# Turning rows by transfers through DRAM and VectorE's 32x32 transposition instead of by TensorE, in a fused attention, MLP and mixture-of-experts kernel

## The chip, the cores and the metric

The kernel runs on one core of a Trainium2 chip. The metric is the device time of one execution in microseconds (us), median of three runs. TensorE does the matrix products, VectorE and ScalarE empty the products' accumulators and prepare operands, GpSimd (POOL in the profile) splits weights and issues the indirect transfers, and SyncE (SP) issues the other transfers.

## The reference

Three blocks follow one another on 2304 tokens of width 512, all in float32:

```python
attn = softmax over a window of 64 earlier keys (4 x 576 tokens, 8 heads of 64)   # _attn_ref
x = relu(x @ w_in) ** 2 @ w_out                                                  # 512 -> 2048 -> 512
logits = x @ w_gate + log1p(exp(x @ w_noise)) * noise                            # 8 experts
top2, weights = the two largest logits of a token, softmax over them
for e in range(8):
    mask = tokens that chose e
    out[mask] += weight * (relu(x[mask] @ w1[e]) @ w2[e])                        # 512 -> 1024 -> 512
```

## The kernel before

Every product runs in three float32r terms: each operand is kept as a high part (a copy) and a low part (source less the high part), and TensorE does high·high, high·low and low·high. Weights are split into the two parts by `split`: ScalarE copies, GpSimd subtracts (L148, L149).

**The middle block** works in groups of 384 tokens. `L1` (L329) and `L2` (L346) alternate over 16 hidden blocks. Each group's output rows `x2` (three tiles of 128 tokens) go to DRAM, to `x2d` (L375). Attention of the next group and `gating` of the group before run between these products as fillers. `gating` needs the tokens turned, channels on the partitions: four TensorE transposes for each tile (L387) into an accumulator, from which ScalarE copies the high part (L390) and VectorE subtracts the low part (L391) into `x2T`. Then come the gating product with `wgn`, which holds the weights of both gates (L396), a copy `lgT` (L399), three small transposes back (L403), a chain of small VectorE operations that finds the top two and flags them in `cm`, and the counting products on `cm` (L457 to L459).

**The expert block** runs in passes: expert 0 in two (its first three tiles, then two), then experts 1 to 7 with five tiles each (624 slots). A pass runs `m2_L1` (L329 with 312 or 256 columns) and the second product (L346) over eight hidden blocks f. While one expert runs, `prep` makes the next one's `x2T`: indirect gathers of the chosen rows from `x2d` into `gx` by GpSimd (L546), then for each tile four TensorE transposes (L564), the copy (L566) and the subtraction (L567). `prep` is added as a filler at f = 4 (`PNF`). `stage2` loads the next expert's weights block by block (L533, L535) on SP. ScalarE and VectorE empty each hidden block (L582, L583), and `finish` gathers the sums so far (`gy`), adds (L594) and scatters back (L552).

A scheduler of the framework moves instructions within each engine, so the order on an engine is not the order of the code. All plain transfers of this stretch share SP's queue.

Of the kernel before, what the change touches and what calls it, by code (L numbers as in the profile page):

```python
# [8 lines left out]
F32 = mybir.dt.float32  # L9
# [4 lines left out]
AF = mybir.ActivationFunctionType  # L14
OP = mybir.AluOpType
AX = mybir.AxisListType
REST = 4
NREST = 1
P0F = 6
PNF = 4  # L20
LB = 4
QB = 0
KT = 1
# [17 lines left out]
def moe_kernel(ctx, tc, q, k, v, w_in, w_out, wg, wn, noise, w1, w2, out):  # L41
    nc = tc.nc
    B, H, S, D = q.shape
    N, DM = out.shape
    E, _, F2 = w1.shape
    F = w_out.shape[0]
    NCC = DM // 128
# [3 lines left out]
    TG = 384  # L51
# [30 lines left out]
    def ps(tag):  # L82
        return psum.tile([128, 512], F32, name=tag, tag=tag, bufs={"o": 3, "h": 2, "att": 3}[tag])
# [37 lines left out]
    def late_consts():  # L121
        nc.gpsimd.iota(iotas, pattern=[[1, 128]], base=0, channel_multiplier=0,
                       allow_small_or_imprecise_dtypes=True)
        nc.gpsimd.iota(pidx, pattern=[[0, 1]], base=0, channel_multiplier=1,
                       allow_small_or_imprecise_dtypes=True)
        nc.gpsimd.memset(ones, 1.0)
        nc.gpsimd.affine_select(out=tri, in_=ones, pattern=[[1, 128]], compare_op=OP.is_gt,
                                fill=0.0, base=0, channel_multiplier=-1)
        nc.gpsimd.memset(base, 0.0)
        nc.gpsimd.memset(cnt, 0.0)  # L130
        nc.gpsimd.memset(table, 0.0)
        wf = stg.tile([128, 512], F32, name="cv", bufs=CVB)[:, :NCC * 2 * E].rearrange("p (c e) -> p c e", c=NCC)
        nc.sync.dma_start(wf[:, :, :E], wg.rearrange("(c p) e -> p c e", p=128))
        nc.sync.dma_start(wf[:, :, E:], wn.rearrange("(c p) e -> p c e", p=128))
        nc.scalar.activation(wgn[:, :, 0], wf, AF.Copy)
        nc.gpsimd.tensor_sub(wgn[:, :, 1], wf, wgn[:, :, 0].bitcast(F32))
        nt = stg.tile([N // 128, 128 * E], F32, name="st", bufs=STB)
        nc.sync.dma_start(nt, noise.rearrange("(t p) e -> t (p e)", p=128))
        pn = ps("att")
        for e in range(E):  # L140
            nc.tensor.transpose(pn[:, e * (N // 128):(e + 1) * (N // 128)],
                                nt.rearrange("t (p e) -> t e p", e=E)[:, e], ident[:N // 128, :N // 128])
        nc.vector.tensor_copy(noi.rearrange("p t e -> p e t"),
                              pn[:, :N // 128 * E].rearrange("p (e t) -> p e t", e=E))
# [231 lines left out]
                x2s[g].append(x2)  # L376


    GAT = {}

    def gating(g):
        gat = GAT["pool"]
        x2T = gat.tile([128, 2, NCC, TG], F32R, name="x2T")
        for t in range(TT):
            pt = ps("att")
            for c in range(NCC):
                nc.tensor.transpose(pt[:, 128 * c:128 * c + 128], x2s[g][t][:, 128 * c:128 * c + 128], ident)  # L387
            tl = slice(128 * t, 128 * t + 128)
            src = pt.rearrange("p (c n) -> p c n", c=NCC)
            nc.scalar.activation(x2T[:, 0, :, tl], src, AF.Copy)  # L390
            nc.vector.tensor_sub(x2T[:, 1, :, tl], src, x2T[:, 0, :, tl].bitcast(F32))  # L391
            yield
        pl = ps("att")
        for c in range(NCC):
            for i in range(2):
# [134 lines left out]
    def stage2(e, f):  # L530
        pool = M2["stg"]
        st = pool.tile([128, 1024], F32, name="st2")
        nc.sync.dma_start(st[:, :512].rearrange("p (c f) -> p c f", c=NCC),  # L533
                          w1[e, :, 128 * f:128 * f + 128].rearrange("(c p) f -> p c f", p=128))
        nc.sync.dma_start(st[:, 512:], w2[e, 128 * f:128 * f + 128, :])  # L535
        ws = []
        for i in range(2):
            w = ringa.tile([128, 2, 512], F32R, name="w")
            split(w, st[:, 512 * i:512 * i + 512])
            ws.append(w)  # L540
        return ws
# [14 lines left out]
    def prep(tiles, xT):  # L556
        for j, i in enumerate(tiles):
            gather(gx[j], x2d, i)
        for _ in range(NREST if len(tiles) == 2 else 0):
            yield  # L560
        for j, i in enumerate(tiles):
            pt = ps("att")
            for c in range(NCC):
                nc.tensor.transpose(pt[:, 128 * c:128 * c + 128], gx[j][:, 128 * c:128 * c + 128], ident)  # L564
            src = pt.rearrange("p (c n) -> p c n", c=NCC)
            nc.scalar.activation(xT[:, 0, :, 128 * j:128 * j + 128], src, AF.Copy)  # L566
            nc.vector.tensor_sub(xT[:, 1, :, 128 * j:128 * j + 128], src,  # L567
                                 xT[:, 0, :, 128 * j:128 * j + 128].bitcast(F32))
            yield

    w2s = {}
# [57 lines left out]
    def add_fill(gen, n):  # L629
        fill.append(gen)  # L630
        left[0] += n
# [50 lines left out]
    for g in range(NG):  # L682
        drain()
        if g == 1:
            stg.release()
            GAT["pool"] = tc.alloc_tile_pool(name="gat", bufs=1)
        if g == NG - 1:
            att.release()
            gxp = tc.alloc_tile_pool(name="gxp", bufs=1, side="right")
            gx = []  # L690
            for j in range(CT):
                t = gxp.tile([128, DM], F32, name=f"gx{j}")
                nc.vector.memset(t, 0.0)
                gx.append(t)
            M2["stg"] = tc.alloc_tile_pool(name="stg2", bufs=2, side="right")
        if g + 1 < NG:
            add_fill(att_group(g + 1), 4 * UG)
        for f in range(NF):
            if g == NG - 1 and f >= 2 and f - 2 < NF2:
                w2s[0, f - 2] = stage2(0, f - 2)  # L700
            if g == 0 and f == NF - 3:
                late_consts()
            if g == 1 and f == 8:
                clear_out()
            slots = 2 * (NF - f)
            L1(g, f)
            filler(-(-left[0] // slots))
            if prev:
                L2(*prev)
            if f == 0 and g > 0:  # L710
                add_fill(gating(g - 1), 6 + 2 * REST)
            if f == NF - 1 and g == NG - 1:
                drain()
                index_tables(0, TT)
                xA = xtp.tile([128, 2, NCC, TG], F32R, name="xT")
                add_fill(prep(list(range(TT)), xA), TT)
            filler(-(-left[0] // (slots - 1)))
            prev = (g, f)
# [10 lines left out]
    for n, (e, tiles) in enumerate(passes):  # L729
# [15 lines left out]
        for f in range(NF2 + 1):  # L745
# [17 lines left out]
            if f == (P0F if n == 0 else PNF) and n + 1 < len(passes):  # L763
                nt = passes[n + 1][1]
                if n == 0:
                    xnext = xtp.tile([128, 2, NCC, 256], F32R, name="xT")
                else:
                    xnext = M2["x"].tile([128, 2, NCC, 128 * CT], F32R, name="x2T2")
                add_fill(prep(nt, xnext), len(nt))
        drain()  # L770
        if e > 0 and not gy:
            for j in range(CT):
# [116 lines left out]
```

## Time and profile before

| what | value |
|---|---|
| median of three runs | 1056.31 us (1056.09 to 1056.58) |
| the profiled execution | 1056.97 us, its span from first to last instruction 1055.0 us |
| mean granted TensorE clock | 0.991 of full speed |
| TensorE busy | 1017.3 us, 96% of the span |
| VectorE, ScalarE, GpSimd busy | 509.1, 417.8, 409.6 us (48%, 40%, 39%) |
| rows moved by indirect gather into `gx` | 40 tiles of 256 KB, 3.4 us each from issue to landing |

A line such as `L564 PE MATMUL att<-ident,gx ... x160 | 23.6, 272` reads: line 564 of the kernel, TensorE, matrix multiplication into the accumulator `att`, 160 of them, 23.6 us busy in all, 272 ns the mean of one. Consecutive products overlap, so the mean of one is longer than what one adds to the chain. The brackets in a timeline give the idle time before an instruction and what ended it.

### The profile page before, as it was taken

Reading aid. Unit: us, or ns where it says so; the run is one execution under the profiler, and the core shown is the slowest. Engines: PE = TensorE matmul, PEld = TensorE weight load, DVE = VectorE, ACT = ScalarE, POOL = GpSimd, SP = SyncE. Lnnn points to the kernel's source line nnn. Section 1 sums busy time; section 2 is a strip of 40 time slices with the busy share of each in tenths; the row PEclk is TensorE's granted clock in tenths of the full one; section 3 lists DMA queues with packets and bytes.
Section 4 is the critical chain, followed back from the end, with each engine's and each line's share of the span. In section 5 each row is a group of like instructions: output and inputs, shape, how many; then the busy total and the mean of one; then the engine's idle time right before and its main releaser. Section 6 shows DMA issues by size and latency. Waiting matters only on the chain.

```text
span 1055.0 us, 16793 instructions
## 1 busy us (share of the span) xinstructions
PE 1017.3 (96%) x6120; PEld 899.5 (85%) x6120; DVE 509.1 (48%) x1195; ACT 417.8 (40%) x1037; POOL 409.6 (39%) x405
## 2 busy tenths in 40 slices
PE   8877799999999999999989999999999999999997
PEld 6656688889888988888878889998898998998996
DVE  7999977436645744753773642131312222231312
ACT  4664555335434443533532335332333233333210
POOL 3565631100200210110260059766565756565411
PEclk9998999999999999999999999999999999999999
DMA  9655546212112111211330326444343444443111
GB/s 200 178 160 159 164 105 235 47 30 70 39 33 78 31 39 48 54 32 23 111 111 1 110 92 194 154 140 150 117 156 106 153 134 132 128 134 121 46 47 47
DMA packets 148736, 108.33 MB, mean 103 GB/s; under 512 B 85753, under 2 KB 126713, under 8 KB 148651
## 3 DMA queue, kind: packets, MB, share of 16 engines
q1 hardware_dynamic: 139451, 80.09, 26.8%
q0 software_dynamic: 9200, 27.14, 8.2%
q8 instruction: 50, 0.82, 0.3%
q14 instruction: 35, 0.29, 0.1%
HBM read 89.27 MB, written 20.48 MB: 104 GB/s over the span
## 4 chain that ended last, share of the span: by engine, by line
PE 78%; DVE 10%; issue 6%; ACT 2%; POOL 1%; DMA 1%; POOLq 0%; SPq 0%; ACTq 0%; DVEq 0%
PE h L329 34%; PE o L346 27%; PE att L346 6%; PE att L255 2%; PE att L283 2%; DVE x L161 2%; PE att L564 2%; DVE x L162 1%; PE att L272 1%; DVE h L359 1%; DVE x L160 1%; PE att L396 1%; ACT P L265 1%; DVE r L358 1%; POOL out_dram L552 1%
## 5 line engine op out<-in xcount | busy, mean ns | idle before, releaser
L346 PE MATMUL o<-w,h 128*128 128x512 f32 x1488 | 391.4, 401 | 16.8 <-DVE h L359 12.4
L346 PEld LDWEIGHTS o<-w,h 128*128 128x128 f32 x1488 | 269.8, 189 | 74.4 <-DVE h L359 16.2
L329 PE MATMUL h<-xT,w 128*128 128x384 f32 (+1 forms) x1344 | 262.8, 343 | 3.2 <-DVE xT L287 1.9
L329 PEld LDWEIGHTS h<-xT,w 128*128 128x128 f32 x1344 | 230.4, 191 | 8.6 <-POOL w L149 2.5
L149 POOL TENSOR_TENSOR w<-st,w 128x512 fp32r<-128x512 f32 x128 | 165.1, 1301 | 104.6 <-ACT w L148 66.5
L329 PE MATMUL h<-x2T,w 128*128 128x312 f32 x1344 | 201.4, 306 | 0.0
L329 PEld LDWEIGHTS h<-x2T,w 128*128 128x128 f32 x1344 | 195.8, 188 | 3.6
L583 DVE SCALAR_TENSOR_TENSOR h<-h 128x312 fp32r<-128x312 f32 (+2 forms) x128 | 61.9, 483 | 272.7 <-ACT h L582 272.7
L148 ACT ACTIVATE w<-st 128x512 fp32r<-128x512 f32 x128 | 80.8, 631 | 191.3 <-PE att L346 119.7
L268 POOL TENSOR_TENSOR P<-P,stat 128x384 f32<-128x384 f32 x48 | 41.7, 871 | 219.4 <-DVE stat L267 103.9
L356 ACT ACTIVATE r<-h 128x384 f32<-128x384 f32 x96 | 46.7, 486 | 142.6 <-PE h L329 123.3
L582 ACT ACTIVATE h<-h 128x312 fp32r<-128x312 f32 (+2 forms) x128 | 54.4, 425 | 116.5 <-PE h L329 116.5
L346 PE MATMUL att<-w,h 128*128 128x512 f32 (+1 forms) x336 | 94.3, 393 | 0.0
L358 DVE TENSOR_TENSOR r<-r 128x384 f32<-128x384 f32 x80 | 53.0, 662 | 69.9 <-ACT h L357 68.6
L346 PEld LDWEIGHTS att<-w,h 128*128 128x128 f32 (+1 forms) x336 | 61.0, 181 | 15.4
L359 DVE TENSOR_TENSOR h<-r,h 128x384 fp32r<-128x384 f32 x96 | 60.5, 630 | 4.9 <-POOL r L358 2.2
L546 POOL DMA_INDIRECT gx<-x2d,ix x40 | 40.9, 1022 | 49.2 <-PE att L564 40.8
L552 POOL DMA_INDIRECT out_dram<-y,ix x35 | 34.4, 984 | 44.1 <-DVE y L594 37.2
L357 ACT ACTIVATE h<-r 128x384 fp32r<-128x384 f32 x96 | 50.2, 523 | 1.5
L265 ACT ACTIVATE P<-P,stat 128x128 f32<-128x128 f32 x96 | 37.6, 392 | 28.1 <-DVE stat L263 23.6
L149 POOL TENSOR_TENSOR w<-x,w 128x512 fp32r<-128x512 f32 x24 | 35.4, 1479 | 27.0 <-ACT w L148 26.8
L546 POOL DMA_INDIRECT gy<-out_dram,ix x35 | 35.6, 1016 | 19.8 <-issue 19.7
(208 smaller groups left out, 988.1 us busy)
## 6 DMA issues: line engine op xcount, KB each, us to landing
st<-in_moe_w_dram SPq DMA_DIRECT2D x128, 256.0 KB, 3.1
st<-in_moe_w_in_dram SPq DMA_DIRECT2D x16, 512.0 KB, 4.3
st<-in_moe_w_out_dram SPq DMA_DIRECT2D x16, 512.0 KB, 3.6
vn<-in_v_dram SPq DMA_DIRECT2D x110, 64.0 KB, 2.2
x2d<-x SPq DMA_DIRECT2D x18, 256.0 KB, 2.7
out_dram<-x SPq DMA_DIRECT2D x1, 4608.0 KB, 15.3
qn<-in_q_dram SPq DMA_DIRECT2D x40, 96.0 KB, 2.5
kn<-in_k_dram SPq DMA_DIRECT2D x28, 128.0 KB, 2.8
```

What stands on the lines that cost most here:

```text
L148: nc.scalar.activation(dst[:, 0], src, AF.Copy)
L149: nc.gpsimd.tensor_sub(dst[:, 1], src, dst[:, 0].bitcast(F32))
L265: nc.scalar.activation(P[:, j], src[:, j], AF.Exp, bias=st[:, j, 0:1], accum_out=st[:, j, 1:2])
L329: nc.tensor.matmul(p[:, :n], w[:, wi, 128 * c:128 * c + 128], x[:, xi, c], start=(c == 0 and i == 0), stop=(c == NCC - 1 and i == 2))
L346: nc.tensor.matmul(o[t][:hs.shape[1]], hs, w[:, wi], start=(first and i == 0 and hi == 0 and wi == 0), stop=(last and i == len(steps) - 1 ...
L356: nc.scalar.activation(r, ph[:, :TG], AF.Relu)
L357: nc.scalar.activation(h[:, 0], r, AF.Square)
L358: (nc.vector if g else nc.gpsimd).tensor_mul(r, r, r)
L359: nc.vector.tensor_sub(h[:, 1], r, h[:, 0].bitcast(F32))
L546: nc.gpsimd.indirect_dma_start(out=dst, out_offset=None, in_=src[:, :], in_offset=bass.IndirectOffsetOnAxis(ap=slot[i][0][:dst.shape[0]], ...
L582: nc.scalar.activation(h[:, 0, a:a + m], ph[:, :m], AF.Relu)
L583: nc.vector.scalar_tensor_tensor(h[:, 1, a:a + m], ph[:, :m], 0.0, h[:, 0, a:a + m].bitcast(F32), op0=OP.max, op1=OP.subtract)
```

## The change

It has two halves. In `gating` of groups 0 to 4 and in the preparation of experts 1 to 7, no TensorE transpose is issued. Instead the rows (for the experts: the gathered rows, after a store to a DRAM buffer `xg`) are read back by four transfers for each tile, each of 32 partitions, 4 pieces of 512 bytes for each; VectorE then transposes each 32x32 block, ScalarE copies the high part and VectorE subtracts the low one, now from a buffer in SBUF rather than from an accumulator. After these steps partition p holds the channels 4p to 4p+3, where it held p, p+128, p+256 and p+384. So `wgn` and the first weights of experts 1 to 7 are loaded in that arrangement too. The gating of the last group (g = 5) keeps the TensorE transposes, on every fourth channel. Expert 0 is unchanged. The preparation of the next expert is added at f = 2 instead of 4, in more steps.

```diff
-PNF = 4
+PNF = 2
...
-        nc.sync.dma_start(wf[:, :, :E], wg.rearrange("(c p) e -> p c e", p=128))
+        nc.sync.dma_start(wf[:, :, :E], wg.rearrange("(p c) e -> p c e", p=128))
...
+    def turned_rows(raw, src, row):
+
+        for a in range(4):
+            nc.sync.dma_start(raw[32 * a:32 * a + 32].rearrange("p (q d) -> p q d", q=4),
+                              src[row:row + 128, 128 * a:128 * a + 128].rearrange("(q i) d -> i q d", i=32))
+
+    def turn(xT, tmp, raw):
+        nc.vector.transpose(tmp.rearrange("p (c q i) -> p q c i", c=NCC, q=4),
+                            raw.rearrange("p (q j c) -> p q c j", q=4, c=NCC))
+        src = tmp.rearrange("p (c n) -> p c n", c=NCC)
+        nc.scalar.activation(xT[:, 0], src, AF.Copy)
+        nc.vector.tensor_sub(xT[:, 1], src, xT[:, 0].bitcast(F32))
...
-        for t in range(TT):
-            pt = ps("att")
-            for c in range(NCC):
-                nc.tensor.transpose(pt[:, 128 * c:128 * c + 128], x2s[g][t][:, 128 * c:128 * c + 128], ident)
...
+        if g < NG - 1:
+
+
+            raws = [hw.tile([128, DM], F32, name="x2", bufs=3) for _ in range(TT)]
+            for t, raw in enumerate(raws):
+                turned_rows(raw, x2d, TG * g + 128 * t)
+            for _ in range(2):
+                yield
+            for t, raw in enumerate(raws):
+                turn(x2T[:, :, :, 128 * t:128 * t + 128], gat.tile([128, DM], F32, name="tb"), raw)
+                yield
+        else:
...
+                    nc.tensor.transpose(pt[:, 128 * c:128 * c + 128], x2s[g][t][:, c::NCC], ident)
...
-                          w1[e, :, 128 * f:128 * f + 128].rearrange("(c p) f -> p c f", p=128))
+                          w1[e, :, 128 * f:128 * f + 128].rearrange("(p c) f -> p c f" if e else "(c p) f -> p c f", p=128))
...
+    def prep_turned(tiles, xT):
+
+        for j, i in enumerate(tiles):
+            gather(gx[j], x2d, i)
+        for _ in range(2):
+            yield
+        xg = dram.tile([128 * len(tiles), DM], F32, name="xg", bufs=2)
+        raws = [hp2.tile([128, DM], F32, name="y", bufs=CT) for _ in tiles]
+        for j in range(len(tiles)):
+            nc.sync.dma_start(xg[128 * j:128 * j + 128, :], gx[j])
+        yield
+        for j, raw in enumerate(raws):
+            turned_rows(raw, xg, 128 * j)
+        for _ in range(2):
+            yield
+        for j, raw in enumerate(raws):
+            turn(xT[:, :, :, 128 * j:128 * j + 128], gx[j], raw)
             yield
...
-                add_fill(gating(g - 1), 6 + 2 * REST)
+                add_fill(gating(g - 1), 8 + 2 * REST)
...
                 if n == 0:
                     xnext = xtp.tile([128, 2, NCC, 256], F32R, name="xT")
+                    add_fill(prep(nt, xnext), len(nt))
                 else:
                     xnext = M2["x"].tile([128, 2, NCC, 128 * CT], F32R, name="x2T2")
-                add_fill(prep(nt, xnext), len(nt))
+                    add_fill(prep_turned(nt, xnext), len(nt) + 5)
```

**TensorE, the gating of group 1 inside group 2.** The names are those of the section on the kernel; `kT`, `qbd`, `qn`, `kn` and `P` belong to attention. Before:

```order
L387 MATMUL att<-ident,x_2690 128x128 x4
L329 MATMUL h<-xT,w 128x384 x12
L255 MATMUL att<-kT,qbd_106 128x128 x3
L396 MATMUL att<-x2T,wgn 32x384 x8
L346 MATMUL o<-w,h 128x512 x9
L234 MATMUL att<-ident,qn 128x96 x2
L236 MATMUL att<-ident,kn 128x128 x2
L403 MATMUL att<-ident,lgT 128x32 x3
```

And now:

```order
L329 MATMUL h<-xT,w 128x384
L422 MATMUL att<-x2T,wgn 32x384
L329 MATMUL h<-xT,w 128x384 x4
L272 MATMUL att<-ident,P 128x128 x2
L422 MATMUL att<-x2T,wgn 32x384 x7
L272 MATMUL att<-ident,P 128x128
L329 MATMUL h<-xT,w 128x384 x4
L429 MATMUL att<-ident,lgT 128x32 x3
```

The four transposes of each tile are gone. Between the last gating product and the small transposes back stood nine products of `L2` and four transposes of attention; now one transpose and four products of `L1` stand there.

**ScalarE, the end of expert 0's second pass and the start of expert 1.** `st` are loaded weights being split, `h` with 256 columns is expert 0's, with 312 columns expert 1's, and `x<-o,wt` scales expert 0's rows. Before:

```order
L582 ACTIVATE h<-h 128x256
L566 ACTIVATE x2T_6758<-att 128x4x128
L148 ACTIVATE w<-st_6893 128x512
L597 ACTIVATE x_6908<-o,wt_6508 128x512
L148 ACTIVATE w<-st_6893 128x512
L597 ACTIVATE x_6910<-o,wt_6508 128x512
L582 ACTIVATE h<-h 128x312 x2
```

And now:

```order
L627 ACTIVATE h<-h 128x256
L389 ACTIVATE x2T_6726<-gx_5532 128x4x128
L148 ACTIVATE w<-st_6826 128x512 x2
L642 ACTIVATE x_6949<-o,wt_6538 128x512
L148 ACTIVATE w<-st_6860 128x512 x2
L642 ACTIVATE x_6951<-o,wt_6538 128x512
L148 ACTIVATE w<-st_6897 128x512 x2
L148 ACTIVATE w<-st_6934 128x512
L627 ACTIVATE h<-h 128x312
```

Seven weight copies now stand between the last turned tile and the first hidden block of expert 1, where two stood.

On TensorE the same place read before:

```order
L564 MATMUL att<-ident,gx_5508 128x128 x4
L346 MATMUL o<-w,h 128x512 x12
L329 MATMUL h<-x2T_6758,w 128x312 x48
L346 MATMUL o<-w,h 128x512 x6
L346 MATMUL att<-w,h 128x512 x2
```

And now:

```order
L346 MATMUL o<-w,h 128x512 x12
L329 MATMUL h<-x2T_6726,w 128x312 x24
L346 MATMUL o<-w,h 128x512 x3
L329 MATMUL h<-x2T_6726,w 128x312 x24
L346 MATMUL o<-w,h 128x512 x3
```

The first three products that need expert 1's first hidden block now follow its first 24 products, where they followed 48.

**SP, one of the later expert passes, now.** Each L559 and L561 pair loads one block of weights; before, only such pairs (L533, L535) stood here.

```order
L559 DMA st_8244<-in_moe_w_dram 128x4x128
L561 DMA st_8244<-in_moe_w_dram 128x512
L382 DMA y<-xg 32x4x128 x2
L559 DMA st_8315<-in_moe_w_dram 128x4x128
L561 DMA st_8315<-in_moe_w_dram 128x512
L382 DMA y<-xg 32x4x128 x18
L559 DMA st_8401<-in_moe_w_dram 128x4x128
L561 DMA st_8401<-in_moe_w_dram 128x512
L559 DMA st_8459<-in_moe_w_dram 128x4x128
L561 DMA st_8459<-in_moe_w_dram 128x512
L606 DMA xg<-gx_5524 128x512
```

The twenty reads of the five tiles stand among the first weight loads of the pass, and the stores of the next expert's gathered rows later in it.

## Rows read from the trace of the kernel before

**Rows 1.** The page: busy time, share of the span, instructions of each engine.

```profile
PE 1017.3 (96%) x6120; PEld 899.5 (85%) x6120; DVE 509.1 (48%) x1195; ACT 417.8 (40%) x1037; POOL 409.6 (39%) x405
```

**Rows 2.** Windows, expert pass 2: us, busy by engine, clock, DMA share, GB/s.

```profile
706.06:763.50 57.44, 57.44 (x334) 51.87 (x334) 14.76 (x28) 18.56 (x37) 35.82 (x32) 1.00 0.44 136
```

**Rows 3.** The chain that ended last, 760 to 800: start, us, what.

```profile
763.42 6.86 PE h L329 x48
...
790.97 1.40 PE o L346 x6
...
797.89 0.44 PE att L564 x4
```

**Rows 4.** Groups by line: the TensorE transposes of tiles.

```profile
L564 PE MATMUL att<-ident,gx 128*128 128x128 f32 x160 | 23.6, 272 | 0.3 <-DMA gx<-x2d,ix 0.3
L387 PE MATMUL att<-ident,x 128*128 128x128 f32 x72 | 10.8, 272 | 0.0
```

**Rows 5.** Groups by line: operations on 128x512 elements.

```profile
L567 DVE TENSOR_TENSOR x2T<-att,x2T 128x512 fp32r<-128x512 f32 x35 | 24.2, 692 | 35.7 <-ACT x2T L566 35.4
L148 ACT ACTIVATE w<-st 128x512 fp32r<-128x512 f32 x128 | 80.8, 631 | 191.3 <-PE att L346 119.7 <-PE h L329 61.0 <-PE o L346 9.0
```

**Rows 6.** Transfers: KB each, median us from issue to landing.

```profile
vn<-in_v_dram SPq DMA_DIRECT2D x110, 64.0 KB, 2.2
x2d<-x SPq DMA_DIRECT2D x18, 256.0 KB, 2.7
gx<-x2d,ix POOLq DMA_INDIRECT x40, 3.4
```

**Rows 7.** SP's timeline: issue time of transfers.

```profile
768.39 0.38 SPq L533 DMA_DIRECT2D st<-in_moe_w_dram  x1
272.54 1.77 SPq L204 DMA_DIRECT2D vn<-in_v_dram  x3
227.63 10.07 SPq L204 DMA_DIRECT2D vn<-in_v_dram  x9
```

**Rows 8.** Timelines of GpSimd, TensorE and VectorE where expert 1 is prepared.

```profile
624.25 1.00 POOL L546 DMA_INDIRECT gx<-x2d,ix  x1 [0.30 <-PE o L346]
631.57 11.29 POOL L149 TENSOR_TENSOR w<-st,w 128x512 fp32r<-128x512 f32 x9 [2.39 <-PE o L346]
635.05 1.55 PE L346 MATMUL o<-w,h 128*128 128x512 f32 x6
648.42 7.03 PE L329 MATMUL h<-x2T,w 128*128 128x312 f32 x48
646.38 0.42 DVE L583 SCALAR_TENSOR_TENSOR h<-h 128x256 fp32r<-128x256 f32 x1 [0.96 <-ACT h L582]
```

**Rows 9.** GpSimd, VectorE at 550 us, and all of line 358: min/median/max ns.

```profile
550.65 3.77 POOL L149 TENSOR_TENSOR w<-st,w 128x512 fp32r<-128x512 f32 x3
550.88 3.97 DVE L358 TENSOR_TENSOR r<-r 128x384 f32<-128x384 f32 x1 [2.66 <-ACT h L357]
L358 DVE TENSOR_TENSOR r<-r x80: 534/559/3966, 152.6 to 580.7; 128x384 f32<-128x384 f32 x80
```

**Rows 10.** TensorE's timeline, gating of group 1.

```profile
256.22 0.37 PE L403 MATMUL att<-ident,lgT 32*128 32x32 f32 x3
267.01 0.18 PE L457 MATMUL att<-cm,tri 128*128 128x24 bf16 x1
```

**Rows 11.** VectorE's timeline there: the copy and the last flag.

```profile
254.41 0.54 DVE L399 COPY lgT<-att 32x384 f32<-32x384 f32 x1
264.54 0.15 DVE L452 TENSOR_TENSOR cm<-cm 128x8 bf16<-128x8 bf16 x1
```

**Rows 12.** TensorE's timeline, gating of group 4.

```profile
520.35 0.37 PE L403 MATMUL att<-ident,lgT 32*128 32x32 f32 x3
531.02 0.19 PE L457 MATMUL att<-cm,tri 128*128 128x24 bf16 x1 [1.52 <-DVE cm L449]
532.43 0.17 PE L458 MATMUL att<-cm,ones 128*128 128x24 bf16 x1 [1.23 <-DVE cm L452]
```

More of the change, by code (lines that the diff above doesn't have):

```diff
@@ L132, in late_consts @@
         wf = stg.tile([128, 512], F32, name="cv", bufs=CVB)[:, :NCC * 2 * E].rearrange("p (c e) -> p c e", c=NCC)
-        nc.sync.dma_start(wf[:, :, :E], wg.rearrange("(c p) e -> p c e", p=128))
-        nc.sync.dma_start(wf[:, :, E:], wn.rearrange("(c p) e -> p c e", p=128))
+        nc.sync.dma_start(wf[:, :, :E], wg.rearrange("(p c) e -> p c e", p=128))
+        nc.sync.dma_start(wf[:, :, E:], wn.rearrange("(p c) e -> p c e", p=128))
         nc.scalar.activation(wgn[:, :, 0], wf, AF.Copy)
@@ L383, in gating @@
         x2T = gat.tile([128, 2, NCC, TG], F32R, name="x2T")
-        for t in range(TT):
-            pt = ps("att")
-            for c in range(NCC):
-                nc.tensor.transpose(pt[:, 128 * c:128 * c + 128], x2s[g][t][:, 128 * c:128 * c + 128], ident)
[L388 to L392, printed above, removed]
+        if g < NG - 1:
[8 more added lines that the diff above has]
+        else:
+            for t in range(TT):
+                pt = ps("att")
+                for c in range(NCC):
+                    nc.tensor.transpose(pt[:, 128 * c:128 * c + 128], x2s[g][t][:, c::NCC], ident)
+                tl = slice(128 * t, 128 * t + 128)
+                src = pt.rearrange("p (c n) -> p c n", c=NCC)
+                nc.scalar.activation(x2T[:, 0, :, tl], src, AF.Copy)
+                nc.vector.tensor_sub(x2T[:, 1, :, tl], src, x2T[:, 0, :, tl].bitcast(F32))
+                yield
         pl = ps("att")
@@ L568, in prep @@
                                  xT[:, 0, :, 128 * j:128 * j + 128].bitcast(F32))
+            yield
[8 more added lines that the diff above has]
+            nc.sync.dma_start(xg[128 * j:128 * j + 128, :], gx[j])
+        yield
+        for j, raw in enumerate(raws):
+            turned_rows(raw, xg, 128 * j)
+        for _ in range(2):
+            yield
+        for j, raw in enumerate(raws):
+            turn(xT[:, :, :, 128 * j:128 * j + 128], gx[j], raw)
             yield
```

## The prediction

> **What bounds the kernel now.** I read the busy line first: TensorE works 96% of the span [rows 1]. The windows of an expert pass sharpen this. In 57.44 us TensorE is busy for all 57.44 at full granted clock, while VectorE has 14.76 us of work, ScalarE 18.56, GpSimd 35.82, and the transfers fill 0.44 of the DMA engines [rows 2]. So a pass ends when TensorE has issued its last product, and the chain of waits must run through TensorE: it does, and the four transposes of a tile are a link in it between products, 0.44 us long [rows 3]. The mean of one transpose is 272 ns [rows 4], but the four overlap. Work taken from TensorE is thus time saved, as long as nothing new makes TensorE wait. The rest of my reading looks for places where it would.
>
> **What is removed.** Thirty-five of the 40 tiles behind L564's 160 transposes lose them (expert 0's five keep theirs): 35 x 0.44 = 15.4 us. Of L387's 72, in 18 tiles, 15 tiles lose them; shape and mean are the same [rows 4], so 15 x 0.44 = 6.6 us. Together **-22.0 us**. The last three gating tiles read every fourth channel as a stationary operand. No row shows a strided one; nothing lost is the lower bound, a doubling of the three links (1.3 us) the upper, and I take 0, since 128 columns are loaded in any case.
>
> **What is added, by the piece.** For each turned tile: four reads of 64 KB, one VectorE transposition, a ScalarE copy and a VectorE subtraction; for the experts also a 256 KB store. The nearest read is `vn`, 2.2 us to land [rows 6] and 1.77 us for three to be issued, 0.59 each; the weight load with the same short runs issues in 0.38 [rows 7]. I take 0.5 each. The store is like `x2d`'s, 2.7 us. The ScalarE copy costs 0.63, as L148's does. The subtraction took 0.69 from PSUM [rows 5]; from SBUF I take 0.75. The transposition is shown nowhere; 0.56, the 384-wide operation of [rows 9], is my lower end, twice 0.69 the upper, and 0.7 my value, because it moves as many elements as L567. VectorE's extra is below 1 us a tile, 5 us a pass, against 42 us idle there.
>
> [...]
>
> **Experts 2 to 7: 0.** The gathers and stores for the next expert lie in the pass before, so its reads can go when a pass starts. On SP two of them follow one weight load, and eighteen the next, which was issued 5.0 us into its pass before (768.39, [rows 7]; the pass began at 763.42, [rows 3]). At 0.5 each, the first tile is down about 9 us into the pass and the last at about 17. VectorE's order puts the fifth turn ahead of the eighth eviction of `h`, whose product began 27.5 us into the pass (790.97, [rows 3]); turn, eviction and their copies need some 3 us, so the tile must be down by 24.5. From 5.9 that is 0.9 us a read at the most (5.9 + 18 x 0.9 + 2.2 = 24.3). That slack is the cover; the price without it is the last rival below.
>
> **Expert 1: +5.3 us.** Here nothing can be early. Expert 0's second pass, which ends at 648.42 [rows 8], must hold the whole chain. Its gathers are issued 1.3 us apart, the last (tile 1) at 624.25 [rows 8], tile 0's at 622.95. That one lands 3.4 later, at 626.4, and its store 2.7 after that, at 629.1. Then 20 reads follow at 0.5, four for the first tile, landing 2.2 behind their issue: tile 0 lies ready at about 633.5, and each next one 2 us later. The scheduler has put the turns between VectorE's evictions of `h`. T0 (0.7), the copy (0.6), the subtraction (0.75) and the eviction of the fourth `h` behind it (0.42) end at 636.1, while the product that needs this `h` started at 635.05 before [rows 8]: 1.05 us of waiting.
>
> That is the lower bound for this part. GpSimd runs nine weight splits without a pause from 631.57, 1.25 us each [rows 8], and a subtraction of two SBUF operands can be shut out by them: at 550.65 three splits took 3.77 us, and the VectorE subtraction that started with them took 3.97 where the median of its line is 0.56 [rows 9]. One split lost brings the wait to about 2.9 us. Shut out through six splits, it would come to 5.6. I take 2.9: the median of that line shows that most operations meet no block at all.
>
> [...]
>
> The second wait comes where expert 1 begins. Its later weight loads lie behind the reads on SP, so ScalarE has seven weight copies of 0.63 [rows 5] and two row scalings, taken at 0.69 like L567, between the last turned tile and the first 312-wide `h`: 5.8 us. That last tile is transposed behind expert 0's last eviction of `h`, which ended at 646.8 [rows 8], and copied by 648.2 on the clock of before; the run of copies then ends at 654.0 and the first `h`, at 0.42, at 654.4. The three products that need it now follow 24 products of the new expert and not 48, so TensorE reaches them at 648.42 + half of 7.03 [rows 8], 651.9. The wait is about 2.4 us. Bounds: 0, if the weight copies fit between the turns after all, and 5.8, if all of them fall on the path. Both waits together: 2.9 + 2.4 = **+5.3**, bounds 1.0 and 11.4.
>
> **Gating of groups 0 to 4.** The rows of group g-1 come back from `x2d` while group g runs, and and its three tiles need a store (2.7), twelve reads (6.0), a landing (2.2) and the last turn (2.1), 13.0 us. By the new order six or seven blocks of products stand ahead of the gating's seven, some 14 us (12 products of 384 columns take 12 x 7.03 / 48 x 384 / 312 = 2.2 us by [rows 8]), so it just fits; a loss of 0 to 1 in each group. After it, the copy of `lgT` (0.54, [rows 11]) has only about 0.8 us of products on TensorE to hide behind, where nine of `L2` stood; it fits, barely. Then the flags: the last one stands ready at 264.54 [rows 11], 8.3 us behind the transposes at 256.22, and the counting product came at 267.01 [rows 10], 2.3 us later; the new order has 1.5 us less between them, so 0.8 is left. Four groups at 0.3, nearer the lower bound since each step by itself fits: **+1.2**, bounds 0 and 4.
>
> Group 4's gating (in group 5) is tighter. There VectorE is late already: the counting products waited 1.52 + 1.23 us [rows 12]. Before, 8.9 us of products and attention stood between the small transposes and them; by the new order 6.0 remain, so the wait can grow by up to 2.85. It can also vanish (-2.75), if the flags no longer meet GpSimd's splits. I take **+2.0**.
>
> **Sum.** -22.0 + 5.3 + 1.2 + 2.0 = -13.5. The profiled execution took 1056.97, so 1043.5 on its scale; the median of the runs is 0.66 lower: 1042.8, said as **1043**.
>
> **Rivals.** *Full cover.* Every new chain hides, the waits at expert 1 too: 1056.3 - 22.0 = 1034.3. For it: VectorE idles three quarters of a pass [rows 2]. Against it: expert 1's chain needs a store, twenty reads and a landing, 2.7 + 10 + 2.2 = 14.9 us more than before, inside one short pass.
>
> *The lock in every pass.* GpSimd splits weights through most of each pass [rows 2], and of the five subtractions a pass one loses a split (11.29 / 9 = 1.25 us, [rows 8]) where it holds up an `h`, with a little more behind it: 1.5 us in each of six passes, 9 us, so about 1052. [...] For it: the 3.97 us [rows 9]. Against: TensorE has a block of products between an `h` and its use, 3.4 us, which one lost split doesn't eat up.
>
> *Slower: SP's issue.* The twenty reads block the weight loads behind them. Past 0.9 us each a pass loses (issue less 0.9) x 18; at 1.025 us this is 2.25 us in each of six passes, 13.5 in all, and the gain is gone. The profile has one such row: nine `vn` in 10.07 us, 1.12 each [rows 7]. At that price it is 4.0 x 6 = 24 us, and about 6 more at expert 1: 1043 + 24 + 6 = 1073. Against it: 0.59 in the other row, and that those 10.07 us may hold waits.
>
> **How the numbers follow.** My forecast has 0.58, full cover 0.17, the lock 0.14, SP's issue 0.07; 0.04 is left for small gains and for no change. Within 0.2%, 2.1 us, is about what a measurement of this kernel can tell from no change. Faster 0.90, the same 0.03, slower 0.07. The forecast's own range, by its bounds (expert 1 -4.3 to +6.1, gating -6.0 to +3.7, the strided tiles +1.3; not all at once), is 1036 to 1050. To hold 8 in 10 I go from 1034.5, which leaves out the lower half of full cover, to 1051, which leaves out most of the lock and all beyond.
>
> **What would show it.** A pass of experts 2 to 6 lasts 55.2 us in the windows with TensorE busy throughout (55.8 or more with waits: the lock; 59: SP's issue). Around 648 us there are two waits of TensorE, one for VectorE's `h` in expert 0's second pass, one for ScalarE's in expert 1's first block. SP's timeline gives a read in about 0.5 us. VectorE's group of transpositions has a mean near 700 ns, and its subtractions one near 750 with a longest of several splits. A wait ahead of the count products in group 5 of 3 us or more shows the last term. I am wrong if the passes hold waits, or if expert 1's chain takes over 10 us more than I gave it.

## The result, and the profile after

The change made the kernel slower: 1063.7 us (1063.1 to 1064.3, four runs) against 1056.2 us for the kernel before on the same chip. The ratio is 1.0071, with an interval of 1.0054 to 1.0089. The forecast was 1043. The profiled execution took 1064.32 us with a span of 1062.4.

The page's busy line, which answers to [rows 1], shows that TensorE was busy 13 us less, and the kernel still ended 7.4 us later. (It is 13 and not the 22 removed because what stayed took 9 us longer: 2.9 in expert 1's pass, 2.4 in groups 1 to 4, 2.3 in the first stretch, 1.0 in the later passes.)

```profile
PE 1004.1 (95%) x5920; PEld 881.2 (83%) x5920; DVE 571.4 (54%) x1245; ACT 418.0 (39%) x1037; POOL 416.3 (39%) x405
```

To see where the time went I took the start of the same instruction in both traces: ScalarE's copy of an `x2` tile, which ends each group, and the first product of each pass.

| stretch | before, us | after, us | forecast | measured |
|---|---|---|---|---|
| to the end of group 0 | 153.2 | 154.4 | 0 | +1.2 |
| groups 1 to 4 | 354.9 | 356.2 | -4.1 | +1.4 |
| group 5 | 76.3 | 77.9 | +0.7 | +1.7 |
| expert 0, first pass | 39.3 | 39.5 | 0 | +0.1 |
| expert 0, second pass | 24.7 | 26.2 | +0.7 | +1.5 |
| expert 1's pass | 57.6 | 66.0 | +0.2 | +8.4 |
| passes of experts 2 to 6 | 286.9 | 279.5 | -11.0 | -7.3 |
| last pass and end | 62.1 | 62.6 | 0 | +0.5 |

The forecasts add up to -13.5, the measured column to +7.5, within rounding the 7.4 of the spans. The first line is not the change: that stretch took 153.0 to 154.4 in the kernels below, whichever part they held. The windows of the five later passes answer to [rows 2] (same columns):

```profile
720.29:776.27 55.98, 55.42 (x314) 49.73 (x312) 22.08 (x32) 18.51 (x37) 36.90 (x31) 1.00 0.66 186
776.27:832.18 55.91, 55.39 (x314) 49.72 (x313) 22.27 (x32) 18.61 (x37) 37.03 (x31) 1.00 0.60 185
832.18:887.33 55.15, 55.15 (x314) 49.73 (x312) 21.19 (x32) 18.75 (x37) 36.73 (x31) 1.00 0.61 188
887.33:943.34 56.01, 55.42 (x313) 49.74 (x312) 21.16 (x32) 18.74 (x37) 37.04 (x31) 1.00 0.61 187
943.34:999.81 56.47, 55.51 (x314) 49.64 (x312) 23.58 (x32) 18.68 (x37) 31.07 (x26) 1.00 0.38 113
```

One pass of the five, the third, is what the forecast called for: 55.15 us, all of it TensorE. In the others TensorE sits idle for 0.5 to 1.0 us. The list of what TensorE waited for (us in all, times, longest) names the new waits:

```profile
PE h L329 <- DVE h L628: 8.4, 5, 5.8
PE o L346 <- ACT h L627: 5.4, 2, 3.4
PE att L483 <- DVE cm L475: 4.9, 1, 4.9
PE att L422 <- ACT x2T L389: 3.3, 5, 1.0
PE att L485 <- DVE cm L478: 1.8, 4, 0.4
```

The first line is evictions of `h` on VectorE that came late for TensorE's next product. The longest lies in expert 1's pass, where the rows of expert 2 are turned. Timelines of GpSimd (the last gather of expert 2's rows), SP, VectorE and TensorE there:

```profile
656.70 1.02 POOL L572 DMA_INDIRECT gx<-x2d,ix  x1
670.36 3.22 SPq L606 DMA_DIRECT2D xg<-gx  x5
673.66 14.25 SPq L382 DMA_DIRECT2D y<-xg  x20
683.62 1.08 DVE L386 STREAM_TRANSPOSE gx<-y 128x512 f32<-128x512 f32 x1 [11.64 <-DMA y<-xg]
685.39 0.69 DVE L390 TENSOR_TENSOR x2T<-gx,x2T 128x512 fp32r<-128x512 f32 x1 [0.70 <-ACT x2T L389]
686.00 0.47 DVE L628 SCALAR_TENSOR_TENSOR h<-h 128x312 fp32r<-128x312 f32 x1
686.53 6.31 PE L329 MATMUL h<-x2T,w 128*128 128x312 f32 x24 [5.76 <-DVE h L628]
```

The stores of expert 2's rows were issued only at 670.36, 16 us into the pass, behind four weight loads. The first tile lay ready ten microseconds after its first read was issued. VectorE started nothing for 11.64 us before the turn. The eviction of an `h` whose products had ended by 677.33 (24 of them, 3.59 us from 673.74) stood behind it: its high part on ScalarE came at 685.27, right behind the copy of the turned tile, and its low part on VectorE at 686.00. TensorE idled 5.76 us and then ran 24 products in 6.31 us instead of the 3.6 of its other blocks. Windows of 5 us show why (the last three numbers: granted clock, DMA share, GB/s):

```profile
675.00:680.00 5.00, 5.00 (x30) 4.48 (x29) 0.00 (x0) 0.00 (x0) 4.56 (x4) 1.00 1.01 334
680.00:685.00 5.00, 0.77 (x4) 0.28 (x2) 1.08 (x1) 0.27 (x1) 2.50 (x3) 1.00 0.66 139
685.00:690.00 5.00, 3.47 (x13) 3.47 (x14) 4.28 (x6) 2.15 (x5) 2.78 (x3) 0.55 0.66 169
```

After the idle stretch the granted clock was 0.55 over a window; in windows of 1 us it was 0.50 from 686 to 692, 0.84 in the next and 1.00 from 693. Wait (5.8) and clock (2.7) together are 8.5 us. And while the reads were under way the DMA engines were full, a share of 1.01; the chain of waits has this read at 8.05 us:

```profile
675.26 8.05 DMA y<-xg
```

In the pass before, where expert 1 is turned, the chain is the one forecast from the stores on SP to the turn. TensorE's first wait, though, was for ScalarE's high part of `h`, which stood behind ScalarE's copy of the turned tile (from 641.44) and a weight copy. VectorE's low part, which the forecast had as the late one, came only at 643.12, when TensorE already ran again:

```profile
626.94 7.23 SPq L606 DMA_DIRECT2D xg<-gx  x5
636.81 9.33 SPq L382 DMA_DIRECT2D y<-xg  x20
640.26 1.10 DVE L386 STREAM_TRANSPOSE gx<-y 128x512 f32<-128x512 f32 x1 [4.98 <-DMA y<-xg]
642.50 0.36 ACT L627 ACTIVATE h<-h 128x256 fp32r<-128x256 f32 x1
642.91 1.67 PE L346 MATMUL o<-w,h 128*128 128x512 f32 x6 [3.39 <-ACT h L627]
643.12 0.41 DVE L628 SCALAR_TENSOR_TENSOR h<-h 128x256 fp32r<-128x256 f32 x1
659.81 0.96 PE L346 MATMUL o<-w,h 128*128 128x512 f32 x3 [1.97 <-ACT h L627]
```

In a later pass the same pattern is small, and once a subtraction of a turn (L390) that lasts 4.79 us beside GpSimd's splits costs TensorE time. (Subtractions of 1.8 to 2.4 us stand in the other four of these passes too, but no wait of TensorE follows them.) Timelines of TensorE, GpSimd and VectorE:

```profile
731.52 1.10 DVE L386 STREAM_TRANSPOSE gx<-y 128x512 f32<-128x512 f32 x1 [4.93 <-DMA y<-xg]
733.03 1.99 PE L329 MATMUL h<-x2T,w 128*128 128x312 f32 x12 [0.56 <-DVE h L628]
...
962.62 5.04 POOL L149 TENSOR_TENSOR w<-st,w 128x512 fp32r<-128x512 f32 x4
963.42 4.79 DVE L390 TENSOR_TENSOR x2T<-gx,x2T 128x512 fp32r<-128x512 f32 x1 [0.70 <-ACT x2T L389]
968.66 3.70 PE L329 MATMUL h<-x2T,w 128*128 128x312 f32 x24 [0.96 <-DVE h L628]
```

The gating's waits, in group 2 and in group 5, where the last line answers to the two of [rows 12]:

```profile
260.70 0.37 PE L422 MATMUL att<-x2T,wgn 128*32 128x384 f32 x1 [0.57 <-ACT x2T L389]
274.25 0.17 PE L485 MATMUL att<-cm,ones 128*128 128x8 bf16 x1 [0.44 <-DVE cm L478]
541.91 0.19 PE L483 MATMUL att<-cm,tri 128*128 128x24 bf16 x1 [4.88 <-DVE cm L475]
```

The new operation's price, from the groups by line, and the subtraction's spread (min/median/max ns), the experts' above, the gating's below:

```profile
L386 DVE STREAM_TRANSPOSE gx<-y 128x512 f32<-128x512 f32 x35 | 38.1, 1089 | 39.7 <-DMA y<-xg 39.7
```

```profile
L390 DVE TENSOR_TENSOR x2T<-gx,x2T x35: 691/693/4793, 642.1 to 970.3; 128x512 fp32r<-128x512 f32 x35
L390 DVE TENSOR_TENSOR x2T<-tb,x2T x15: 682/691/1139, 164.4 to 527.4; 128x512 fp32r<-128x512 f32 x15
```

### The profile page after: what moved, and what is told of

The parts are those of the page before. It is cut to its first block, busy times and chain, and to the rows that moved or that the text cites. A ratio compares the mean times of both kernels' runs of the same rounds, so it can differ in the third digit from the quotient of the medians.

```text
span 1062.4 us, 16856 instructions
## 1 busy us (share of the span) xinstructions
PE 1004.1 (95%) x5920; PEld 881.2 (83%) x5920; DVE 571.4 (54%) x1245; ACT 418.0 (39%) x1037; POOL 416.3 (39%) x405
## 4 chain that ended last, share of the span: by engine, by line
PE 61%; DVE 15%; issue 9%; DMA 5%; ACT 4%; SPq 3%; POOL 2%; POOLq 1%; DVEq 0%; ACTq 0%
PE h L329 27%; PE o L346 21%; PE att L346 5%; DMA y<-xg 2%; PE att L283 2%; DVE x L161 2%; SPq L382 2%; PE att L255 2%; ACT P L265 1%; DVE h L359 1%; DVE x L162 1%; DVE r L358 1%; PE att L272 1%; POOL out_dram L578 1%; PE att L422 1%
## 5 line engine op out<-in xcount | busy, mean ns | idle before, releaser
L329 PE MATMUL h<-x2T,w 128*128 128x312 f32 x1344 | 204.2, 309 | 8.4 <-DVE h L628 8.4
L329 PEld LDWEIGHTS h<-x2T,w 128*128 128x128 f32 x1344 | 199.3, 191 | 14.8 <-DVE h L628 10.1
L359 DVE TENSOR_TENSOR h<-r,h 128x384 fp32r<-128x384 f32 x96 | 58.1, 605 | 4.6 <-POOL r L358 2.2
L386 DVE STREAM_TRANSPOSE gx<-y 128x512 f32<-128x512 f32 x35 | 38.1, 1089 | 39.7 <-DMA y<-xg 39.7
L389 ACT ACTIVATE x2T<-gx 128x512 fp32r<-128x512 f32 x35 | 22.1, 632 | 79.9 <-DVE gx L386 74.4
L572 POOL DMA_INDIRECT gx<-x2d,ix x40 | 43.9, 1097 | 17.4 <-issue 5.0
L390 DVE TENSOR_TENSOR x2T<-gx,x2T 128x512 fp32r<-128x512 f32 x35 | 40.8, 1166 | 17.7 <-ACT x2T L389 17.7
```

What stands on the lines that cost most here:

```text
L329: nc.tensor.matmul(p[:, :n], w[:, wi, 128 * c:128 * c + 128], x[:, xi, c], start=(c == 0 and i == 0), stop=(c == NCC - 1 and i == 2))
L359: nc.vector.tensor_sub(h[:, 1], r, h[:, 0].bitcast(F32))
L572: nc.gpsimd.indirect_dma_start(out=dst, out_offset=None, in_=src[:, :], in_offset=bass.IndirectOffsetOnAxis(ap=slot[i][0][:dst.shape[0]], ...
```

## The experiments

They ran on other chips than the first measurement, where the kernel before took 1058 to 1062 us, so only ratios to the kernel before on the same chip are compared. Kernels of one group below shared a chip. My theory: TensorE saves what was forecast, and loses it because evictions of `h` stand on VectorE behind turns whose rows are late. The rivals: the transfers themselves (SP's queue, full DMA engines), VectorE's longer work, with subtractions of up to 4.79 us beside GpSimd's splits, or the gating.

**Halves and parts.** `TURNED` is the set of experts that are turned, `GTURN` the gating.

```diff
+GTURN = True        # gating_only: TURNED = ();  experts_only: GTURN = False, TURNED = 1 to 7
+TURNED = ()         # experts_3to7: GTURN = False, TURNED = 3 to 7
...
-                    add_fill(prep_turned(nt, xnext), len(nt) + 5)
+                    add_fill(prep_turned(nt, xnext), len(nt) + 5) if ne in TURNED else add_fill(prep(nt, xnext), len(nt))
```

Gating alone:

> Only the gating of groups 0 to 4 is turned by transfers; all experts keep TensorE's transposes, their weights and the start of their preparation as before. My theory after the result, that the gating's half loses more than it saves (from the two traces: groups 1 to 4 are 1.4 us longer together, group 5 1.7 us): slower than before by 2 to 4 us, about 1059. The rival, that the gating's half gains and the whole loss lies with the experts (-6.6 removed, 1 us of waits in each of four groups, 5.9 in group 5 against 2.75 before): faster by 0 to 2 us, or the 4.9 us wait in group 5 is missing.

Measured 1.0039 (1.0024 to 1.0054), 1066.6 us against 1062.3. The gating's half loses by itself; its 5.0 us wait in group 5 is there. The rival is out.

Experts alone:

> Only experts 1 to 7 are turned; the gating and its weights are as before. By the sum of the pieces of the two traces (pass 1 of expert 0 +1.5, expert 1 +8.4, experts 2 to 6 together -7.3, the last +0.5): slower than before by about 3 us, 1059 to 1060, with the 5.8 us wait of TensorE in expert 1's pass still there. The rival, that this wait is a late effect of the shifted gating ahead: the wait is gone and the kernel is about 6 us faster than before, 1050.

Measured 0.9986 (0.9972 to 0.9999), 1060.7 us. The wait in expert 1's pass is there, 4.97 us, so it is no late effect of the gating. The size was off: 1.5 us faster, not 3 slower.

Experts 3 to 7 alone:

> Only experts 3 to 7 are turned; the gating and experts 1 and 2 are prepared by TensorE as before. Theory, that the loss belongs to the two experts whose gathers cannot lie a pass ahead: faster than before by 7.3 us (five preparations, 1.5 us each), 1049. The rival, that whichever expert is first to be turned pays (its stores and reads start late in any case): a wait of several us in the pass that prepares expert 3, and 1054 or more.

Measured 0.9921 (0.9905 to 0.9938), 8.4 us under the kernel before. The loss of the experts' half belongs to experts 1 and 2; whichever comes first need not pay (the pass that prepares expert 3 has one wait, 0.36 us).

**The chain taken away.**

```diff
-            gather(gx[j], x2d, i)
...
-            nc.sync.dma_start(xg[128 * j:128 * j + 128, :], gx[j])
...
-            turned_rows(raw, xg, 128 * j)
+            turned_rows(raw, x2d, 128 * j)
```

> As the changed kernel, but the gathers of experts 1 to 7 and the stores to xg are left out, and the twenty reads of each expert take the first 640 rows of x2d, which are there long before; turns, copies and subtractions are all there. Theory, that expert 1's and 2's preparation wait for the chain gather, store, read: the waits of 3.4 us in the second pass and 5.8 us in expert 1's pass, with the lower clock behind the latter, are gone, 1047 to 1050. The rival, that VectorE's turns (1.09 us each) and the blocked subtractions are what holds up the eviction of h: waits of several us stay in expert 1's pass, 1056 or more.

Measured 0.9880 (0.9861 to 0.9898), 1049.8 us. That is 12.5 us under the kernel before on this chip, where 6 to 9 were expected (1047 to 1050 against the 1056 of the first chip). From 620 us on TensorE waited for no more than this:

```profile
PE att L593 <- DMA gx<-x2d,ix: 1.6, 2, 0.8
PE h L332 <- DVE h L624: 0.5, 1, 0.5
PE o L349 <- DVE h L624: 0.5, 1, 0.5
```

All 35 turns and the long subtractions were there (one lasted 5.0 us, the median 0.69), so VectorE's work alone is not the cause. But less was transferred too; the next run keeps the transfers.

**The turns later, with the same work.** First the changed kernel again, then its late form:

> The changed kernel once more, its order of instructions the same, so that it is timed on the same chip as the next three. Theory and rival both expect 0.4 to 0.9% over the kernel before; the 5.8 us wait in expert 1's pass stands in its trace if it belongs to the program and not to one execution.

Measured 1.0047 (1.0033 to 1.0061), with a wait of 5.62 us at the same product.

```diff
+        with tc.issue_after(after) if after is not None else ExitStack():    # after: the last eviction of h so far
+            nc.vector.transpose(
...
-            if nt and f == (P0F if n == 0 else PNT if ne in TURNED else PNF):      # PNT = 2
+            if nt and f == (P0F if n == 0 else PNT if ne == 1 and ne in TURNED else 0 if ne in TURNED else PNF):
...
-        for _ in range(2):        # between gathers and stores
+        for _ in range(1 if late else 2):
...
-        for _ in range(2):        # between reads and turns
+        for _ in range(4 if late else 2):
```

> As the changed kernel, but the turns for experts 2 to 7 are issued on VectorE behind the tenth, twelfth and fourteenth eviction of h of the pass (they stood from the third or sixth on), and gathers, stores and reads are added two blocks earlier. The work is the same. Theory, that h queues on VectorE behind a turn whose rows have not landed: the 5.8 us wait and the lower clock behind it in expert 1's pass (8.6 us) and the 0.5 to 1.0 us waits of the later passes are gone, 12 us less than the changed kernel, ratio to before 0.995. The rival, that the transfers themselves hold the pass up (weight loads behind the reads on SP, DMA engines over full): the wait moves to another place of the pass and the time stays within 3 us of the changed kernel.

Measured 0.9945 (0.9931 to 0.9960): 11 us less than the changed kernel beside it. After the first block of expert 1, TensorE has no wait in the trace to the end. Two of its passes:

```profile
713.52:768.68 55.16, 55.16 (x314) 49.73 (x312) 19.46 (x32) 19.07 (x37) 36.70 (x31) 1.00 0.63 189
768.68:823.83 55.15, 55.15 (x313) 49.72 (x312) 19.44 (x32) 19.06 (x37) 36.64 (x31) 1.00 0.62 187
```

With the DMA share as high as in the changed kernel, every pass from expert 2 to expert 6 takes 55.15. This is the run that decides: the same work and the same transfers cost TensorE nothing in these passes once no turn stands ahead of an eviction of `h` before its rows have landed. What it doesn't separate is the turns' place from that of the transfers, which also moved forward. In expert 1's pass (from 656.48) the stores came 5.8 us into the pass and not 16.1, the reads 11.1 and not 19.4:

```profile
662.23 2.91 SPq L612 DMA_DIRECT2D xg<-gx  x5
667.62 9.97 SPq L385 DMA_DIRECT2D y<-xg  x20
```

By my estimate, with the 8.05 us of the slowest read, the first tile lay ready some 21 us into that pass, and TensorE needed the eviction at 26.5 in the changed kernel. So there the earlier transfers alone might have done it. So might the turns' place alone: the first turn began 30.5 us into the pass, and in the changed kernel its rows were down at 29.4. No run shows either by itself. For the later passes the run with twice the reads (below) has the answer.

**Late turns for experts 2 to 7, expert 1 and the gating on TensorE.**

> The same late turns for experts 2 to 7; expert 1 and the gating are prepared by TensorE as before. Theory: 6 preparations at 2.2 us, 13.2 us under the kernel before, ratio 0.9875, and no wait of TensorE over 0.3 us in the passes of experts 1 to 6. The rival, that the reads' place on SP delays the weights: waits of 1 us and more for split weights, 0.992 or more.

Measured 0.9878 (0.9856 to 0.9900), as expected; from 640 us on the trace has no wait of TensorE at all. Beside the next-but-one kernel, again:

> The kernel with late turns for experts 2 to 7 and all else on TensorE, timed once more beside the next one: 0.987 to 0.989 of the kernel before.

Measured 0.9882 (0.9861 to 0.9903), 1044.2 us.

**The subtraction on GpSimd.**

```diff
-        nc.vector.tensor_sub(xT[:, 1], src, xT[:, 0].bitcast(F32))
+        nc.gpsimd.tensor_sub(xT[:, 1], src, xT[:, 0].bitcast(F32))
```

> Experts 3 to 7 turned as in the earlier run of that set (ratio 0.9921), but the turns' subtraction is done by GpSimd, not VectorE. Theory, that VectorE's subtraction of two SBUF operands is shut out by GpSimd's weight splits (up to 4.8 us for one): the transpositions and evictions keep their times, no VectorE operation of the passes lasts over 1.2 us, and the wait of about 1 us in the pass of expert 6 is gone, 0.990 to 0.992. The rival, that GpSimd at 5 x 1.3 us more in a pass becomes late with the weights: waits for split weights, 0.994 or more.

Measured 0.9905 (0.9888 to 0.9922). The subtraction takes 1297 ns there, the transposition 1100:

```profile
L393 POOL TENSOR_TENSOR x2T<-gx,x2T 128x512 fp32r<-128x512 f32 x25 | 32.4, 1297 | 0.2
L389 DVE STREAM_TRANSPOSE gx<-y 128x512 f32<-128x512 f32 x25 | 27.5, 1100 | 26.5 <-DMA y<-xg 20.2 <-POOL w L152 5.0 <-issue 0.7
```

No VectorE operation of the passes lasts over 1.12 us, and the wait of 0.96 us in the pass of expert 6 is gone, as the theory has it. But the interval overlaps with that of experts_3to7, and waits of 0.4 and 0.6 us remain, so the price of the long subtractions is not settled by this run; in the trace of the changed kernel it is that one wait of 0.96 us.

**The gating later.**

```diff
+            for _ in range(2):        # behind the turns of groups 0 to 4
+                yield
...
-        for _ in range(REST):
+        for _ in range(REST + 3 if GTURN and g < NG - 1 else REST):
```

> The same, and the gating of groups 0 to 4 is turned by transfers too, but its products stand two steps later behind the turns and its counting products three steps later than in the changed kernel, so that they no longer come before their operands and the eight products stand in one piece. Theory, that the gating's half lost its 6.6 us to TensorE's waits (0.57 and 0.44 us in each of groups 1 to 4, 4.9 us in group 5) and to products cut into pieces: the waits in groups 1 to 4 are gone, that of group 5 is under 1.5 us, and the time is 5 to 7 us below the kernel beside it, 0.982 of the kernel before. The rival, that turning by transfers costs the groups as much elsewhere (VectorE has 1.09 us a tile more, with attention queued behind it): the waits move to products of attention or of L2, and the time stays within 2 us of the kernel beside it.

Measured 0.9835 (0.9816 to 0.9854), 1040.6 us beside 1044.2. A group lasts 87.59 us, where it lasted 88.80 to 88.86 before: the 1.25 us of its three tiles' transposes, and no wait is left in groups 1 to 4. The eight products stand in one piece:

```profile
260.29 1.64 PE L430 MATMUL att<-x2T,wgn 128*32 128x384 f32 x8
```

Two waits have come elsewhere, so the gain over the kernel beside it is 3.6 us by the medians and 5.0 by the ratios, at or under the low end of what was expected. One, 2.7 us at 534.8, is of a product of `L2` in group 5 for VectorE's `h`, the place that the rival named; it stands where the 4.9 us of the counting products were. The other lies in expert 1's pass. There seventeen reads on SP held up the weight loads, a weight copy waited for its load on ScalarE, and the eviction of `h` (its high part on ScalarE, then its low part on VectorE) waited behind that copy:

```profile
652.09 9.86 SPq L385 DMA_DIRECT2D y<-xg  x17
667.17 0.63 ACT L151 ACTIVATE w<-st 128x512 fp32r<-128x512 f32 x1 [9.60 <-DMA st<-in_moe_w_dram]
668.69 3.70 PE L332 MATMUL h<-x2T,w 128*128 128x312 f32 x24 [1.79 <-DVE h L636]
```

It is the same pattern on another engine: an instruction whose data is late stands ahead of an eviction. This kernel is the fastest of all here, 1.65% under the kernel before.

**Expert 1 alone.** `TURNED = (1,)`, gating on TensorE.

> Only expert 1 is turned (early, as in the changed kernel); all else as before. Theory, that expert 1 itself costs the two waits on ScalarE's h seen in the changed kernel's trace (3.4 us in the pass before it, 2.0 us at its own start) less its five transposes (2.2 us), which is also what the prediction had for it (+5.3 - 2.2 = +3.1), and that the 5.8 us wait later in its pass belongs to the preparation of expert 2: 3 us slower than before, ratio 1.003, no wait near 30 us into expert 1's pass. The rival, that this wait comes of expert 1's late weight loads: it stays, and the ratio is 1.008 or more.

Measured 1.0028 (1.0017 to 1.0040). Its passes from expert 1 to the end hold one wait, 1.58 us at the first block, and none 30 us into the pass: that one belongs to expert 2's preparation. The second pass's wait was 4.57 us, but ScalarE had stopped there for another reason (last section), so the 3.4 us are not confirmed by themselves.

**Twice the reads.**

```diff
             turned_rows(raw, xg, 128 * j)
+            turned_rows(raw, xg, 128 * j)
```

> The kernel with late turns for experts 2 to 7 (ratio 0.988), but every read from xg is issued twice, into the same place: 40 reads of 64 KB for each expert instead of 20, 1.3 MB more. Theory, that with the turns behind the tenth eviction the reads have time to spare, and neither SP's issue nor the DMA engines bound a pass: passes of 55.2 to 55.5 us, ratio 0.987 to 0.991. The rival, that the transfers were close to the bound all along: each read at 0.53 us holds the weight loads 10.6 us longer, passes of 57 us and more, 0.997 or more.

Measured 0.9876 (0.9852 to 0.9901). SP's timeline, in a window that opens behind the first two, has 38 of a pass's 40 in one run, and the pass in which they lie (windows) is as long as ever:

```profile
764.85 25.37 SPq L385 DMA_DIRECT2D y<-xg  x38
```

```profile
761.26:816.41 55.15, 55.15 (x314) 49.72 (x313) 21.85 (x33) 18.83 (x37) 36.39 (x32) 1.00 0.68 208
```

So neither the issue on SP nor the DMA engines bound a steady pass, and the prediction's rival of a slower kernel, SP's issue, is out for these passes. The last read was issued 29 us into this pass, where it was 16 us in the changed kernel's passes. With transfers later than there, and no wait, it is the turns' place that counts in the later passes.

## Why the prediction was wrong

**What is removed, -22.0: right.** Passes without a wait take 55.15 us against 57.4, which is five links of 0.45, and late_gating's groups give 0.42 a tile.

**"Experts 2 to 7: 0": this step failed, and it carries 12 of the 21 us between forecast and result.** It has two faults. "The gathers and stores for the next expert lie in the pass before" is not so for expert 2. Its gathers wait for expert 1's turns to free the same `gx` buffers, and the last was issued 2.4 us into expert 1's pass; its stores came 16 us into the pass, since four weight loads stood before them on SP. I took the order of a later pass for all of them. That cost 8.5 us, wait and lower clock. And I took the slack of an `h` from the second product that reads it, and only at the fifth tile. TensorE needs the eviction sooner: the accumulator that it empties is one of two (tag `h`, `bufs` 2), so the next-but-one half block of products waits for it. For the eighth eviction this is 25.8 us into the pass of [rows 3], not 27.5, and for the fourth 12.0: half a block (1.72) behind the starts of the blocks of 24 products at 787.52 and 773.72. In three of the later passes the wait came at the fourth eviction: it stood behind the first turn, whose rows were down at 11.2 us (731.52 less 720.29) and not at 9. In a fourth pass it was the subtraction of 4.79 us. Hence 0.5 to 1.0 us in four of the five passes, with the clock and small change 3.8 us (279.5 less 5 x 55.15). The price for a missing cover was set down only for slow issues on SP, and these took 0.47 to 0.56 us, about as I had it (0.71 in expert 1's pass).

**Expert 1, +5.3: right in sum, by luck in part.** The waits were 3.39 + 1.97 = 5.4. The first came another way than forecast. The chain took 2.5 us longer from the gather at 627.25 to the first turn: the gather 4.9 us instead of 3.4, the store 4.6 instead of 2.7. That tile's subtraction took 1.09 us, 0.4 over the median, and no whole split was lost, although one was in my 2.9; the long subtraction came at a later tile (2.36 us, beside two splits of GpSimd in 2.56). And TensorE waited for ScalarE's high part of `h`, not for VectorE's low one. The 2.9 itself is not worked out: 1.05 and one split of 1.25 make 2.3. The transposition took 1.09 us instead of 0.7, and the subtraction from SBUF 0.69 (median), where I had put 0.75 with no row that shows one.

**Groups 1 to 4, +1.2: mis-sized.** They lost 1.6 us each, 6.3 in all (356.2 for the four against 349.95 in late_gating): 0.57 before the gating product, 0.44 before the counting products, and some 0.5 that no wait shows and by which TensorE's busy time was longer than in late_gating. There the products stand in one piece and not between others; that this is the reason is not shown by itself. My upper bound, 4, was too low, because it left out the order's own cost.

**Group 5, +2.0: near, but under.** The wait before the counting products grew from 2.75 to 4.88 us, and the one at the gating product from 0.4 to 1.03. The stretch was 1.67 us longer although three links of 0.42 were gone from it, so the term measured 2.9.

**Strided transposes, 0: right within 0.1 us.** Their weight loads took 204 ns instead of 140, but the four of a tile took 0.63 us instead of 0.60; the first pass of expert 0, where they end, is 0.1 us longer.

**The rivals.** Full cover is what late turns come near to. What the prediction calls the lock shows in the times: the 3.97 us of [rows 9], a product of `r` with itself and not a subtraction as I called it, beside three splits, and here a subtraction of 4.79 us beside four splits of 5.04 in all. What brings it about, no run shows. In the passes it cost TensorE one wait of 0.96 us, not 9 us. On the slower side I looked at one place, the reads' issue on SP, and the loss came at another; SP's order did cost something at expert 1's pass, in the late stores here and in late_gating's 1.8 us. The range (to 1051) left out that several small losses, each with bounds of its own, go the same way.

## What to carry to other kernels

Work moved off the engine that bounds the kernel is worth its price only if what replaces it stands late enough in the engines' queues: a helper instruction whose data may be late must not stand ahead of an eviction that the bound engine needs (in expert 1's pass that cost 5.76 us of waiting, 8.5 us with the lower clock behind it). Check the first round of a pipelined preparation by itself, since the steady order of the later rounds doesn't hold there, and count the slack of an eviction from the reuse of its accumulator, not from the use of its result. Moving the turns behind the tenth eviction, and their transfers two blocks forward, turned +0.5% into -0.5%, and with expert 1 and the gating left on TensorE into -1.2%.

## What the hardware showed that I had not expected

A VectorE transposition in 32x32 blocks of 128x512 float32 takes 1.09 us (1.07 to 1.11 in 35), against 0.69 for a copy or subtraction of that size.

With the DMA engines full (share 1.01) a 64 KB read took 8.05 us from issue to landing, against a median of 2.6. A weight load of w1 in the new arrangement was issued in 0.55 us, where it took 0.38 [rows 7].

On the later chips ScalarE stood still for 3.6 to 6.2 us at about 627 us in six of the profiled executions, at the first eviction of expert 0's second pass, and the trace names only "remote" as the releaser. It was not there in the two profiles of the first chip. What it is stays open. No trace of the kernel before was taken on those chips, so whether it stood still there too isn't known, and some of the ratios may hold a few us of this. The changed kernel again and its late form both have it (5.1 and 6.0 us), so it does not explain the 11 us between them.
